# Cheaper conversion of float64 weights and a due time for every piece, in a planned attention, mixture-of-experts and gated-convolution kernel

## The chip, the cores and the metric

One core of one Trainium2 chip runs the whole program. The time is device microseconds (us) of one execution; lower is better. Runs of this kernel agree within about 0.2%.

## The reference

Three layers follow one another, for batch 4, sequence 576 and model width 512 (8 heads of 64). The first is a local attention over a band of seven positions plus an attention on queries, keys and values averaged by four. The second is a causal attention with four experts of which each token takes two. The third is a convolution with five taps that gates a linear product.

```python
out_local = softmax(where(|i-j| < 4, q k^T / 8, -1e9)) v
x = repeat(softmax(qd kd^T / 8) vd, 4) + out_local
for e in range(4):
    ye = softmax(causal(x wq[e] (x wk[e])^T / 8)) (x wv[e]) wo[e]
    x2 += gate[e] * ye
gate = 1 / (1 + exp(-sum_k conv_w[k] * x2[t - 4 + k]))
y = (gate * (x2 w_val)) w_out
```

The weights `w_val`, `conv_w` and `w_out` arrive as float64, since each is float32 data times a float64 scalar. All other inputs are float32.

## The kernel before

Each batch goes through `attention` (four pairs of heads, each with loads, a "down" path on averaged data and two groups of band windows), `project` (keys, queries, values and gate logits of the experts), `experts` (scores, exponentials, weights, transposes and values for five blocks T of 128 tokens and two pairs of experts) and `tail` (the products with `wo`, `w_val` and `w_out`, and the convolution). Products of full precision are sums of three TensorE products of split operands (`mm3`, lines 936 to 939).

Nothing is issued while these functions run. They record pieces: some instructions of one engine with an estimated cost, the buffers that they read and write, and a due time. `Plan.order` (line 174) then plays the pieces through a model of the engines and writes out one order for each of them: on each engine the piece with the least due time among those that are ready goes next, where buffers are to be had. Due times come from `PARAMS` by batch and stage; line 151 adds an entry of `NUDGE`, which is empty. `PARAMS` also says which engine takes many of the pieces (`"v_00": "dve"`), and how many PSUM banks or `row` buffers each use may hold (`c_...`, `r_...`). A PSUM bank (`ps`) that is handed on makes its next writer wait until its last reader is done. The engines work through their queues in the written order, so a piece that has to wait holds up everything behind it on its engine.

The float64 conversion is in `chunk` (line 563). A value of 64 bits is loaded as two 32-bit words; nine chunks go this way: four of `w_val` and four of `w_out`, each of 128 by 512 values, and one of 128 by 20 (`conv_w`). Before, a chunk takes these steps:

- VectorE (DVE) shifts the upper word into float32 place and clears the sign (lines 596 and 600); ScalarE (ACT) takes the upper word's absolute value and its sign (604 and 608); DVE zeroes values that are too small (613).
- DVE shifts the lower word and takes the exponent of the result (619, 620); ACT turns the lower word into a scaled float (624).
- GpSimd (POOL) multiplies the two, adds the product to the value and multiplies by the sign (628 to 630).

Places that the prediction names: the scores of the experts (lines 1085 to 1087), the row minimum of the negated scores on DVE (1111), exponentials on ACT (1119), the weights (1152), transposes (1159), the value product (1220); in the attention the down scores (830), the band scores (872), the transposes (839, 884), products with values (853, 902), the sum of the two paths on DVE (910); the results of the last product leave through line 1315.

Of the kernel before, what the change touches and what calls it, by code (L numbers as in the profile page):

```python
# [21 lines left out]
TINY64 = 2.0 ** -15 * 1.125  # L22

# [6 lines left out]
    8, "c_mo": 3, "c_ms": 2, "c_mt": 3, "c_o": 7, "c_s": 5, "c_t": 4, "c_w": 5, "cv_00": 3, "cv_01": 4,  # L30
# [6 lines left out]
    "pool", "k_23": "dve", "k_30": "pool", "k_31": "dve", "k_32": "pool", "k_33": "pool", "kk_00": "own",  # L37
    "kk_01": "load", "kk_02": "load", "kk_03": "load", "kk_10": "load", "kk_11": "own", "kk_12": "own",
    "kk_13": "load", "kk_20": "load", "kk_21": "own", "kk_22": "load", "kk_23": "load", "kk_30": "load",
    "kk_31": "own", "kk_32": "own", "kk_33": "load", "late": 275.02, "m_000": "dve", "m_001": "dve",  # L40
# [54 lines left out]
}  # L95


NUDGE = {
}

# [201 lines left out]
def f32r(n):  # L302
    return max(0.459 * n, 112) / 1000
# [23 lines left out]
def tile_local_attention__then__moe__then__gated_conv(  # L327
# [14 lines left out]
    nc = tc.nc  # L342
# [1038 lines left out]
```

## Time and profile before

| | |
|---|---|
| median of 3 runs | 431.75 us (431.65 to 432.47) |
| the profiled execution | 431.73 us |
| its span, first to last instruction | 430.0 us |
| busy: PE, PE weight loads | 389.1, 330.0 us |
| busy: DVE, ACT, POOL | 347.0, 287.5, 187.1 us |
| HBM traffic | 81 GB/s over the span |

PE is TensorE's matmul side. An engine is busy while at least one of its instructions runs; the granted clock (PEclk) is 1.00 at 2.4 GHz and 0.50 at 1.2 GHz. Idle time of an engine is named after what ended it. Matmuls overlap in the pipeline, so that a busy PE may still lose small amounts of time between matmuls.

### The profile page before, as it was taken

The numbers are of one execution on the slowest core, as the hardware profiler recorded it, in microseconds if no ns is written. First come the engines' busy times: TensorE is split into PE (matmuls) and PEld (weight loads), VectorE is DVE, ScalarE is ACT, GpSimd is POOL, SyncE is SP. The second block draws the span as 40 slices with busy tenths as digits, with TensorE's granted clock in tenths as the row PEclk, the third lists the DMA queues.
The fourth block names the chain that finished last, engine by engine and source line by source line (L and its number), as shares of the span: only waits on it lengthen the run. The fifth ranks groups of instructions, "written<-read, shape, count | busy, mean of one in ns | idle before, by whom it ended". The sixth has DMA issues, their size and how long they took to land.

```text
span 430.0 us, 10150 instructions
## 1 busy us (share of the span) xinstructions
PE 389.1 (90%) x3520; PEld 330.0 (77%) x3520; DVE 347.0 (81%) x1032; ACT 287.5 (67%) x974; POOL 187.1 (43%) x256
## 2 busy tenths in 40 slices
PE   0856699999789999999988999999999999999996
PEld 0545479877467898797976798979788998878996
DVE  6788848989997869999989999877773667698765
ACT  5485765268778763548989875579898636666541
POOL 8365567377276384357743730210322700134220
PEclk9996779999687999999999999999999999999999
DMA  8897524136422200020355431302101000100111
GB/s 210 228 242 225 141 81 136 31 102 183 134 81 75 80 17 14 0 79 29 111 151 142 142 85 58 100 2 69 36 22 63 2 2 2 37 15 1 48 64 63
DMA packets 28595, 35.45 MB, mean 82 GB/s; under 512 B 3328, under 2 KB 18688, under 8 KB 28544
## 3 DMA queue, kind: packets, MB, share of 16 engines
q1 hardware_dynamic: 28544, 34.81, 28.7%
q8 instruction: 28, 0.46, 0.5%
q14 instruction: 23, 0.19, 0.2%
HBM read 30.08 MB, written 4.72 MB: 81 GB/s over the span
## 4 chain that ended last, share of the span: by engine, by line
PE 51%; DVE 24%; ACT 15%; issue 4%; POOL 3%; DMA 3%; POOLq 0%; DVEq 0%; ACTq 0%
PE ps L937 10%; PE ps L938 10%; PE ps L939 10%; ACT p L786 5%; PE ps L1159 4%; PE ps L1220 4%; PE ps L1085 3%; DMA v<-in_vx_dram 3%; DVE mmin L1111 2%; ACT pT L890 2%; PE ps L902 2%; PE ps L830 2%; DVE pe L1152 2%; DVE pT L890 1%; DVE mpT L551 1%
## 5 line engine op out<-in xcount | busy, mean ns | idle before, releaser
L1275 POOL TENSOR_TENSOR row<-row,row 128x256 f32<-128x256 f32 (+1 forms) x52 | 43.5, 838 | 53.9 <-ACT row L1271 43.6
L1119 ACT ACTIVATE pe<-ps,mmin 128x128 f32<-128x128 f32 (+4 forms) x80 | 41.5, 524 | 18.0 <-DVE mmin L1111 14.8
L786 ACT ACTIVATE p<-ps,mx 128x64 f32<-128x64 f32 (+1 forms) x116 | 39.6, 342 | 10.1 <-DVE mx L781 7.1
L937 PE MATMUL ps<-xh,wqk_h 128*128 128x256 f32 (+1 forms) x128 | 41.4, 323 | 0.6 <-ACT mpT L551 0.2
L1280 DVE SCALAR_TENSOR_TENSOR row<-ps,cw,row 128x320 f32<-128x320 f32 (+1 forms) x76 | 38.0, 515 | 4.3 <-POOL row L1275 3.7
L1152 POOL TENSOR_SCALAR pe<-pe,es,gw 128x384 f32<-128x384 f32 (+3 forms) x23 | 14.5, 631 | 59.9 <-DVE es L1132 26.9
L1111 DVE TENSOR_REDUCE mmin<-ps 128x1 f32<-128x128 f32 (+4 forms) x80 | 35.7, 476 | 5.5 <-PE ps L1087 4.8
L937 PE MATMUL ps<-gh,wout_h 128*128 128x256 f32 (+1 forms) x128 | 39.3, 307 | 0.0
L938 PE MATMUL ps<-gl,wout_h 128*128 128x256 f32 (+1 forms) x128 | 37.9, 296 | 0.0
L1159 PE MATMUL ps<-ident,pe 128*128 128x128 f32 x192 | 34.2, 292 | 4.0 <-DVE row L910 1.9
L938 PE MATMUL ps<-xl,wqk_h 128*128 128x256 f32 (+1 forms) x128 | 37.8, 295 | 0.0
L939 PE MATMUL ps<-xh,wqk_l 128*128 128x256 f32 (+1 forms) x128 | 37.8, 295 | 0.0
L939 PE MATMUL ps<-gh,wout_l 128*128 128x256 f32 (+1 forms) x128 | 37.7, 295 | 0.0
L1159 PEld LDWEIGHTS ps<-ident,pe 128*128 128x128 f32 x192 | 22.2, 146 | 9.6 <-POOL pe L1152 2.3
L830 PE MATMUL ps<-kd,qd 128*112 128x144 f32 x96 | 17.6, 327 | 12.3 <-POOL kd L742 10.7
L1220 PE MATMUL ps<-mpT,vE 128*64 128x320 f32 (+4 forms) x224 | 27.3, 377 | 0.0
L872 PE MATMUL ps<-kz,qz 128*64 128x64 f32 x640 | 25.9, 230 | 0.8 <-DMA kz<-in_kT_dram 0.5
L872 PEld LDWEIGHTS ps<-kz,qz 128*64 128x64 f32 x640 | 22.5, 143 | 4.8 <-issue 2.4
L937 PEld LDWEIGHTS ps<-xh,wqk_h 128*128 128x128 f32 x128 | 24.1, 188 | 2.6 <-issue 0.6
L819 POOL TENSOR_TENSOR p<-p,sm 128x256 f32<-128x256 f32 (+2 forms) x19 | 15.6, 828 | 23.5 <-DVE sm L810 19.2
L1271 ACT ACTIVATE row<-ps,cw 128x256 f32<-128x256 f32 (+1 forms) x52 | 24.6, 499 | 1.5 <-POOL row L1275 0.8
L902 PE MATMUL ps<-pT,vw 128*64 128x116 f32 (+1 forms) x320 | 23.0, 284 | 2.8 <-ACT pT L890 1.7
(195 smaller groups left out, 1327.1 us busy)
## 6 DMA issues: line engine op xcount, KB each, us to landing
vw<-in_vx_dram SPq DMA_DIRECT2D x32, 160.0 KB, 3.7
qz<-in_qT_dram SPq DMA_DIRECT2D x32, 144.0 KB, 3.0
kz<-in_kT_dram SPq DMA_DIRECT2D x32, 144.0 KB, 2.9
v<-in_vx_dram SPq DMA_DIRECT2D x16, 288.0 KB
kt<-in_kT_dram SPq DMA_DIRECT2D x10, 288.0 KB, 5.6
out_dram<-o SPq DMA_DIRECT2D x16, 160.0 KB, 1.8
v<-in_w_val_dram SPq DMA_DIRECT2D x4, 512.0 KB
v<-in_w_out_dram SPq DMA_DIRECT2D x4, 512.0 KB, 3.3
```

Of the source, the lines that this page charges most:

```text
L786: nc.scalar.activation(pv()[:, i], sv()[:, i], AF.Exp, scale=scale, bias=mx.t[:n, i:i + 1], accum_out=sums()[:, i:i + 1])
L872: nc.tensor.matmul(s.t[64 * h:64 * h + 64, (w - w0) * 64:(w - w0) * 64 + 64], qb.t[:, h, WQ * w:WQ * w + 64], kz.t[:, h, WQ * w:WQ * w + 6 ...
L902: nc.tensor.matmul(po.t[64 * h:64 * h + 64, q0 - t0:q1 - t0], vw.t[:, a, 64 * h:64 * h + 64], pT.t[:, a - w0 // 2, h].rearrange("p w q -> ...
L937: nc.tensor.matmul(p, ah, bh, start=first, stop=False)
L938: nc.tensor.matmul(p, ah, bl, start=False, stop=False)
L939: nc.tensor.matmul(p, al, bh, start=False, stop=last)
L1111: nc.vector.tensor_reduce(out=m.t[:, a:a + 1], in_=s.t[:, :c1 - c0], op=ALU.min, axis=AX.X)
L1119: nc.scalar.activation(pe.t[:, c0:c1], s.t[:, :c1 - c0], AF.Exp, bias=m.t[:, 0:1], scale=-1.0, accum_out=es.t[:, a:a + 1])
L1159: nc.tensor.transpose(pt.t[:, (nf - 1 - j) * P:(nf - j) * P], pe.t[:, j * P:(j + 1) * P], ident)
L1220: nc.tensor.matmul(av.t[64 * e:64 * e + 64, z:n], vE.t[:kr, j, 2 * pr + e, :], pT.t[:kr, e, k0:k0 + n - z], start=(j == 0), stop=(j == Tl))
L1275: nc.gpsimd.tensor_add(g.t[:, :nn], g.t[:, :nn], g2.t[:, :nn])
L1280: nc.vector.scalar_tensor_tensor(g.t[:, :nn], x2.t[:, k:k + nn], cw.t[:, m, k:k + 1], g.t[:, :nn], op0=ALU.mult, op1=ALU.add)
```

## The change

A chunk is converted in other steps. DVE copies the sign bit from the upper word into the result with bit operations, so that the sign by ACT and the multiplication by POOL go. The lower word's top 23 bits are placed behind the result's own sign and exponent; POOL subtracts the bare exponent, and DVE scales the difference and adds it. For a chunk, DVE has seven instructions where it had five, ACT one where it had three, POOL one where it had three.

`NUDGE` gets 2,763 entries, one due-time shift for each piece. In `PARAMS` 73 of the letters that place a piece on an engine change, and ten numbers, most of them buffer counts; some constants of the planner's model change too.

```diff
     "a_300": 0, "a_301": 0, "a_310": 0, "a_311": 0, "a_320": 1, "a_321": 1, "a_330": 1, "a_331": 1, "c_d":
-    8, "c_mo": 3, "c_ms": 2, "c_mt": 3, "c_o": 7, "c_s": 5, "c_t": 4, "c_w": 5, "cv_00": 3, "cv_01": 4,
+    6, "c_mo": 6, "c_ms": 2, "c_mt": 2, "c_o": 5, "c_s": 7, "c_t": 4, "c_w": 2, "cv_00": 3, "cv_01": 4,
...
 NUDGE = {
+    0: 0.78, 1: 19.2, 2: -1.61, 3: 0.78, 4: -0.14, 5: -7.62, 6: 16.78, 7: 6.98, 8: 0.76, 9: -21.27, 10:
...
-    PATIENCE, AHEAD, HEAD = 0.1, 4.0, {"dve": 0.13, "pool": 0.05}
+    PATIENCE, AHEAD, HEAD = 0.05, 0.0, {"dve": 0.13, "pool": 0.05}
...
 def f32r(n):
-    return max(0.459 * n, 112) / 1000
+    return max(0.459 * n + 5, 112) / 1000
...
-        raw, a0, a1, ss = buf("v4"), buf("o"), buf("o"), buf("o")
+        raw, a0, a1 = buf("v4"), buf("o"), buf("o")
...
-        @piece("act", act(n, True), [raw, ss], [ss])
-        def _():
-            nc.scalar.activation(ss.t[:, :n], words(1).bitcast(F32), AF.Sign)
-
-        @piece("dve", vec(n), [a0, a1], [f], kind="port")
+        @piece("dve", vec(3 * n, 3, 0) + 0.2, [raw, a0, a1], [f, a0, a1], kind="port")
         def _():
 
             nc.vector.scalar_tensor_tensor(f.t[:, :n], part(1).bitcast(F32), TINY64, part(0).bitcast(F32),
                                            op0=ALU.is_ge, op1=ALU.mult)
-
-
-        @piece("dve", vec(n, 2), [raw, f, a0, a1], [a0, a1], kind="port")
-        def _():
-            nc.vector.tensor_single_scalar(part(0), words(0), 8, op=ALU.logical_shift_right)
-            nc.vector.tensor_single_scalar(part(1), f.t[:, :n].bitcast(I32), 0x7F800000, op=ALU.bitwise_and)
-
-        @piece("act", act(n, True), [a0], [a0])
-        def _():
-            nc.scalar.activation(a0.t[:, :n], part(0), AF.Copy, scale=2.0 ** -44)
-
-        @piece("pool", gps(3 * n, 3), [a0, a1, ss, f], [f, a0])
-        def _():
-            nc.gpsimd.tensor_mul(a0.t[:, :n], a0.t[:, :n], a1.t[:, :n])
-            nc.gpsimd.tensor_add(f.t[:, :n], f.t[:, :n], a0.t[:, :n])
-            nc.gpsimd.tensor_mul(f.t[:, :n], f.t[:, :n], ss.t[:, :n])
+            nc.vector.scalar_tensor_tensor(whole(), words(1), SIGN, whole(), op0=ALU.bitwise_and, op1=ALU.bitwise_or)
+
+            nc.vector.tensor_single_scalar(part(1), whole(), SIGN | 0x7F800000, op=ALU.bitwise_and)
+            nc.vector.scalar_tensor_tensor(part(0), words(0), 9, part(1), op0=ALU.logical_shift_right, op1=ALU.bitwise_or)
+
+        @piece("pool", gps(n), [a0, a1], [a0])
+        def _():
+            nc.gpsimd.tensor_sub(a0.t[:, :n], a0.t[:, :n], a1.t[:, :n])
+
+        @piece("dve", vec(n), [a0, f], [f], kind="port")
+        def _():
+            nc.vector.scalar_tensor_tensor(f.t[:, :n], a0.t[:, :n], 2.0 ** -20, f.t[:, :n], op0=ALU.mult, op1=ALU.add)
         return f
...
-        @piece("dve", 1.66, [L], [ge, gw, gm], kind="port")
+        @piece("dve", 1.9, [L], [ge, gw, gm], kind="port")
```

How instructions move is seen at two places. In the changed kernel a line number is larger by 388 up to the conversion and by 380 behind it (L1159 is L1539, L902 is L1282, L1111 is L1491). `ps_63` is a PSUM bank, `pe_129` a buffer of exponentials, `ah` and `wo` the operands of a product of the tail, `qb`, `kh` and `kl` those of the scores of the last block of tokens.

**First place: PE in batch 0, the transposes of block T = 3 (four matmuls on `pe_129` and `pe_130`).** Before:

```order
L902 MATMUL ps_63<-pT_96,vw_77 64x116 x6
L937 MATMUL ps_69<-kh_118,qb_116 128x288
L938 MATMUL ps_69<-kl_120,qb_116 128x288
L939 MATMUL ps_69<-kh_118,qb_116 128x288
L1098 LDWEIGHTS identb
L1098 MATMUL ps_69<-cmask_160,identb 128x64
L1159 MATMUL ps_63<-ident,pe_129 128x128 x4
L1159 MATMUL ps_70<-ident,pe_130 128x128 x4
```

Now:

```order
L1478 MATMUL ps_70<-cmask_160,identb 128x64
L1317 MATMUL ps_69<-ah_146,wo_h 128x260
L1318 MATMUL ps_69<-al_148,wo_h 128x260
L1319 MATMUL ps_69<-ah_146,wo_l 128x260
L1317 MATMUL ps_69<-ah_146,wo_h 128x260
L1318 MATMUL ps_69<-al_148,wo_h 128x260
L1319 MATMUL ps_69<-ah_146,wo_l 128x260
L1539 MATMUL ps_63<-ident,pe_129 128x128 x4
L1317 MATMUL ps_68<-ah_146,wo_h 128x260
L1318 MATMUL ps_68<-al_148,wo_h 128x260
L1319 MATMUL ps_68<-ah_146,wo_l 128x260
L1539 MATMUL ps_70<-ident,pe_130 128x128 x4
```

Before, the transposes write bank `ps_63`, which the product with values (L902) filled five matmul rows earlier and which DVE must empty (L910) first. Now `ps_63` was last written 38 rows earlier, by transposes of the attention, and products of the tail stand ahead of both groups of transposes.

**Second place: DVE in batch 0, around the row minimum for block T = 2 and the first chunk of `w_out`.** Before:

```order
L791 TENSOR_TENSOR p_93<-ps_63,mx_82 128x384
L735 TENSOR_TENSOR qd_73<-row_99 64x3x48
L1111 TENSOR_REDUCE mmin_132<-ps_69 128x1
L1111 TENSOR_REDUCE mmin_133<-ps_70 128x1
L799 TENSOR_REDUCE ps_63<-p_93 128x6
L596 TENSOR_SCALAR o_152<-v_76 128x512
L1128 TENSOR_SCALAR es_139<-es_139 128x1
```

Now:

```order
L1171 TENSOR_TENSOR p_93<-ps_68,mx_82 128x384
L997 SCALAR_TENSOR_TENSOR o_154<-o_153,o_152 128x512
L999 SCALAR_TENSOR_TENSOR o_154<-v_76,o_154 128x512
L1001 TENSOR_SCALAR o_153<-o_154 128x512
L1002 SCALAR_TENSOR_TENSOR o_152<-v_76,o_153 128x512
L1491 TENSOR_REDUCE mmin_132<-ps_63 128x1
L1491 TENSOR_REDUCE mmin_133<-ps_70 128x1
```

Before, the two row minima (L1111) stand ahead of the conversion; now four of the conversion's instructions (L997 to L1002) stand ahead of them (L1491).

## Rows read from the trace of the kernel before

**Rows 1.** The page's head and its busy times by engine.

```profile
span 430.0 us, 10150 instructions
...
PE 389.1 (90%) x3520; PEld 330.0 (77%) x3520; DVE 347.0 (81%) x1032; ACT 287.5 (67%) x974; POOL 187.1 (43%) x256
```

**Rows 2.** Stretches: us, busy PE PEld DVE ACT POOL (instructions), PEclk, DMA share, GB/s.

```profile
20.00:40.00 20.00, 11.97 (x142) 9.11 (x139) 17.21 (x39) 14.29 (x54) 10.46 (x14) 0.88 1.01 252
...
100.00:120.00 20.00, 17.41 (x151) 11.63 (x150) 18.96 (x69) 15.06 (x64) 9.55 (x15) 0.76 0.54 158
120.00:140.00 20.00, 17.32 (x127) 13.16 (x126) 16.55 (x48) 17.29 (x56) 13.44 (x14) 0.81 0.23 70
...
220.00:240.00 20.00, 16.53 (x204) 13.23 (x204) 18.54 (x54) 19.00 (x77) 7.37 (x9) 1.00 0.54 152
...
420.00:430.00 10.00, 6.41 (x42) 5.88 (x41) 5.40 (x12) 1.86 (x4) 0.15 (x1) 1.00 0.20 67
```

**Rows 3.** Timeline of PE: start, us, instruction, in brackets idle before and releaser.

```profile
10.70 1.78 PE L830 MATMUL ps<-kd,qd 128*112 128x144 f32 x6 [10.70 <-POOL kd L742]
...
108.67 0.45 PE L839 MATMUL ps<-ident,p 112*72 112x112 f32 x3 [1.08 <-ACT mpT L551]
...
113.78 1.24 PE L853 MATMUL ps<-pdT,vd 72*64 72x144 f32 x8 [1.04 <-ACT pe L1119]
...
125.45 1.21 PE L1159 MATMUL ps<-ident,pe 128*128 128x128 f32 x8 [1.86 <-DVE row L910]
...
129.61 1.11 PE L1159 MATMUL ps<-ident,pe 128*128 128x128 f32 x4 [0.71 <-POOL pe L1152]
...
225.71 0.74 PE L839 MATMUL ps<-ident,p 112*72 112x112 f32 x6 [1.38 <-DVE sm L806]
...
229.85 0.41 PE L884 MATMUL ps<-ident,p 128*128 128x128 f32 x2 [1.48 <-ACT pT L890]
```

**Rows 4.** Timeline of DVE just ahead of the idle PE at 125.45.

```profile
124.89 0.50 DVE L910 TENSOR_TENSOR row<-ps,od 128x348 f32<-128x348 f32 x1
```

**Rows 5.** Timeline of PE: the eight matmuls of L853 at the full clock.

```profile
98.98 0.72 PE L853 MATMUL ps<-pdT,vd 72*64 72x144 f32 x8
```

**Rows 6.** Groups by line and shape: busy us, mean ns of one, idle before, releasers.

```profile
L613 DVE SCALAR_TENSOR_TENSOR o<-o,o 128x512 f32<-128x512 f32 x8 | 6.1, 768 | 0.3 <-ACT o L604 0.3
...
L619 DVE TENSOR_SCALAR o<-v 128x512 int32<-128x512 int32 x8 | 3.8, 478 | 0.1
...
L620 DVE TENSOR_SCALAR o<-o 128x512 int32<-128x512 int32 x8 | 4.3, 542 | 0.0
...
L608 ACT ACTIVATE o<-v 128x512 f32<-128x512 f32 x8 | 5.4, 670 | 0.6 <-POOL o L630 0.6
...
L624 ACT ACTIVATE o<-o 128x512 f32<-128x512 int32 x8 | 5.1, 632 | 4.1 <-DVE o L619 4.1
...
L628 POOL TENSOR_TENSOR o<-o,o 128x512 f32<-128x512 f32 x8 | 10.2, 1274 | 16.5 <-ACT o L624 7.9 <-ACT ah L551 6.3 <-DVE ps L799 1.3
L629 POOL TENSOR_TENSOR o<-o,o 128x512 f32<-128x512 f32 x8 | 10.2, 1276 | 0.6
L630 POOL TENSOR_TENSOR o<-o,o 128x512 f32<-128x512 f32 x8 | 10.4, 1304 | 0.6
```

**Rows 7.** Line 596, the conversion's first step: ns min/median/max, first and last start.

```profile
L596 DVE TENSOR_SCALAR o<-v x9: 414/454/1192, 5.0 to 153.5; 128x512 int32<-128x512 int32 x8, 128x20 int32<-128x20 int32 x1
```

**Rows 8.** Groups by line and shape: a piece of which five go to POOL.

```profile
L750 DVE TENSOR_TENSOR v<-v 72x512 f32<-72x512 f32 x13 | 9.9, 762 | 0.7 <-DMA v<-in_vx_dram 0.6
```

**Rows 9.** Timeline of DVE: the same two instructions, without and beside a POOL instruction.

```profile
8.26 0.62 DVE L735 TENSOR_TENSOR qd<-row 64x144 f32<-64x144 f32 x2
...
13.65 1.57 DVE L735 TENSOR_TENSOR qd<-row 64x144 f32<-64x144 f32 x2
```

**Rows 10.** Timeline of POOL, the instruction that ran beside the second of these.

```profile
13.28 1.46 POOL L630 TENSOR_TENSOR o<-o,o 128x512 f32<-128x512 f32 x1
```

**Rows 11.** Timeline at the end: the four last results leave PSUM.

```profile
425.15 1.81 DVE L1315 TENSOR_SCALAR o<-ps 128x320 f32<-128x320 f32 x4 [0.93 <-PE ps L939]
```

More of the change, by code (lines that the diff above doesn't have):

```diff
@@ L22 @@
 TINY64 = 2.0 ** -15 * 1.125
+SIGN = -0x80000000
 PARAMS = {
@@ L33 @@
     "f1": 122.88, "f2": 399.89, "f3": 539.51, "fl0": 8.06, "fl1": 78.77, "fl2": 166.61, "fl3": 48.67,
[3 rows of a table removed]
[L37 to L40, printed above, removed]
[22 rows of a table removed]
@@ L63 @@
-    "dve", "q_02": "pool", "q_03": "dve", "q_10": "pool", "q_11": "pool", "q_12": "pool", "q_13": "pool",
-    "q_20": "dve", "q_21": "dve", "q_22": "pool", "q_23": "dve", "q_30": "dve", "q_31": "pool", "q_32":
-    "dve", "q_33": "dve", "qe_00": "dve", "qe_01": "dve", "qe_10": "dve", "qe_11": "dve", "qe_20": "act",
[5 rows of a table removed]
-    "dve", "v_02": "dve", "v_03": "dve", "v_10": "pool", "v_11": "dve", "v_12": "pool", "v_13": "dve",
-    "v_20": "dve", "v_21": "dve", "v_22": "dve", "v_23": "dve", "v_30": "dve", "v_31": "pool", "v_32":
@@ L73 @@
-    "dve", "v_33": "dve", "ve_0": "dve", "ve_1": "act", "ve_2": "act", "ve_3": "dve", "w_000": "pool",
[12 rows of a table removed]
-    "wl_o": "dve", "wl_out": "pool", "wl_qk": "dve", "wl_vg": "pool", "wq": 826.51, "wt": 25.89, "xl_000":
-    "pool", "xl_001": "pool", "xl_010": "dve", "xl_011": "dve", "xl_020": "pool", "xl_021": "dve",
-    "xl_030": "pool", "xl_031": "dve", "xl_100": "pool", "xl_101": "pool", "xl_110": "pool", "xl_111":
-    "dve", "xl_120": "dve", "xl_121": "pool", "xl_130": "dve", "xl_131": "pool", "xl_200": "dve",
[5 rows of a table removed]
[2 rows of a table added]
@@ new lines @@
+    "pool", "k_11": "pool", "k_12": "pool", "k_13": "pool", "k_20": "pool", "k_21": "dve", "k_22": "pool",
[3 rows of a table added]
+    "own", "kk_32": "own", "kk_33": "load", "late": 275.02, "m_000": "dve", "m_001": "dve", "m_00d":
+    "dve", "m_010": "dve", "m_011": "act", "m_01d": "dve", "m_020": "act", "m_021": "dve", "m_02d": "act",
[20 rows of a table added]
+    "act", "pt_21": "act", "pt_30": "act", "pt_31": "dve", "q_00": "dve", "q_01": "dve", "q_02": "pool",
+    "q_03": "dve", "q_10": "pool", "q_11": "pool", "q_12": "pool", "q_13": "pool", "q_20": "dve", "q_21":
@@ new lines @@
+    "dve", "q_22": "pool", "q_23": "dve", "q_30": "pool", "q_31": "pool", "q_32": "pool", "q_33": "pool",
[7 rows of a table added]
+    "dve", "v_22": "pool", "v_23": "dve", "v_30": "pool", "v_31": "pool", "v_32": "dve", "v_33": "pool",
[12 rows of a table added]
+    "pool", "w_316": "pool", "w_317": "dve", "w_318": "dve", "wl": 207.52, "wl_o": "dve", "wl_out":
+    "pool", "wl_qk": "dve", "wl_vg": "pool", "wq": 826.51, "wt": 25.89, "xl_000": "pool", "xl_001":
+    "pool", "xl_010": "dve", "xl_011": "dve", "xl_020": "dve", "xl_021": "pool", "xl_030": "pool",
@@ L95 @@
+    "xl_031": "dve", "xl_100": "pool", "xl_101": "pool", "xl_110": "pool", "xl_111": "dve", "xl_120":
+    "dve", "xl_121": "pool", "xl_130": "dve", "xl_131": "dve", "xl_200": "dve", "xl_201": "dve", "xl_210":
+    "pool", "xl_211": "pool", "xl_220": "dve", "xl_221": "pool", "xl_230": "dve", "xl_231": "pool",
[4 rows of a table added]
 }
 NUDGE = {
[387 rows of a table added]
 }
@@ L591, in _, with whole @@
             nc.sync.dma_start(out=place(raw.t[:, :2 * n].bitcast(I32)), in_=rows(I32))
-        @piece("dve", vec(n / 2, 1), [raw], [a0, a1, ss], kind="port")
+        def whole():
+            return f.t[:, :n].bitcast(I32)
+        @piece("dve", vec(n, 2), [raw], [a0, a1], kind="port")
         def _():
             nc.vector.tensor_scalar(part(0), words(1), 0x08000000, 3, op0=ALU.bitwise_xor, op1=ALU.logical_shift_left)
-        @piece("dve", vec(n / 2, 1), [a0], [a0], kind="port")
-        def _():
             nc.vector.tensor_single_scalar(part(0), part(0), 0x7FFFFFFF, op=ALU.bitwise_and)
```

481 rows, old and new, of tables (NUDGE, PARAMS) are left out of this document.

## The prediction, as it was put on record

> **What bounds the kernel now.** I read the busy times first. PE is busy 389.1 of 430.0 us and DVE 347.0; no other engine reaches 300 [rows 1]. So PE sets the end, and what can be won is its 40.9 us of idle time and the time it runs at the lower clock. The matmuls themselves stay: PE has the same 2,875 rows in both orders.
>
> Next come the stretches [rows 2]. From 20 to 40 us PE works only 11.97 of 20.00 us while the DMA share is 1.01: 8.03 us of idle time belong to transfers. At the end PE is idle 10.00 - 6.41 = 3.59 us while the last results leave. From 100 to 140 us the granted clock is 0.76 and then 0.81, and 1.00 at 220 to 240. DVE is nearly full where the clock is low: 18.96 of 20.00 us.
>
> Then the timeline of PE [rows 3], which names what its idle time waits for. 10.70 us lie at the head, ended by POOL's `kd`. Six other gaps are shown: 1.08, 1.04, 1.86 and 0.71 between 108 and 130 us, 1.38 and 1.48 at 225 to 230; together 7.55. What is left is 40.9 - 10.70 - 3.59 - 7.55 = 19.06 us in smaller gaps, of which the transfers' 8.03 make 11.03 that an order of work could fill.
>
> The gap of 1.86 ends with L910 on DVE, which starts at 124.89 and takes 0.50 [rows 4]: the transposes L1159 wait for the bank that L910 empties. The 0.71 four us later waits for POOL's weights (L1152). The clock has a price in the same timeline: eight matmuls of L853 take 1.24 us at 113.78 [rows 3], and 0.72 at 98.98 [rows 5], a factor of 1.72 between the lower level (1.2 GHz) and the full one (2.4).
>
> **The change, part by part.**
>
> *The first place (batch 0, T = 3).* The order puts six products of the tail ahead of the transposes and three more between their two groups, and takes the bank's last use 38 rows back. The nearest row for such products: six matmuls of 144 columns took 1.78 us [rows 3], 2.06 ns a column; six of 260 are 3.2 us, or 3.2 / 1.72 = 1.9 if that row stood at the lower clock; three are 1.6 or 0.93. Both cover 1.86 and 0.71. I count both gaps as gone: **-2.57 us**; bounds 0 (the products' own operand `ah`, which comes next if late, holds PE instead) and -2.57. The products were taken from a later place; what they covered there is in the rivals.
>
> *The other shown gaps.* At 113.78 the product L853 waits for exponentials. In the new order what stands before it still reads a bank filled just ahead (L1233, two rows behind its transposes), so I leave 1.04. The two at 225 and 229 stay: there the transposes L1219 (L839 before) stand four rows behind their own scores. The 1.08 at 108.67 waits for an operand's copy on ACT; no reason to count it. Cost 0 for all, bounds -4.98 (1.08 + 1.04 + 1.38 + 1.48) and 0.
>
> *The clock from 100 to 140.* With two levels, 0.76 over 20 us is 2 x 0.24 x 20 = 9.6 us at the lower, and 0.81 is 7.6: 17.2 us, which at full clock would be 17.2 / 1.72 = 10.0. So 7.2 us can come back, and nothing less than 0. PE idles just before and inside this stretch at four places; two of the four go, so I take half: **-3.6 us**.
>
> *The rest of the schedule.* Over the whole of the orders, between the scores of a block and its transposes stood a median of 9 other pieces on PE, now 11, about a fifth more time for the exponentials and weights in between. A fifth of the 11.03 us: **-2.2 us**, bounds 0 and -11.0. The first 40 us are the transfers' (the same 183 of them), and I expect nothing there; at the head PE waits for `kd` behind the same POOL steps, 0.
>
> *The conversion.* On DVE a chunk loses L619 and L620 (478 + 542 ns) and gains three instructions of the form of L613 (768 each) and one like L620 (542) [rows 6]: +2,846 - 1,020 = +1.83 us, for eight wide chunks +14.6. The narrow ninth is left out, being 20 columns of 512. The masking forms are new. As bounds I take 478 ns, the shortest row of the pass, hence 8 x (3 x 0.478 + 0.542 - 1.020) = +7.7, and 1,192 ns, the longest L596 [rows 7], hence +24.8. ACT loses 670 + 632 a chunk, 10.4 in all; POOL loses two of three steps, 1,274 + 1,304, 20.6 in all. The chain of a chunk behind L613 was 0.478 + 0.542 + 0.632 + 3.854 = 5.5 us and becomes 0.768 + 0.542 + 0.768 + 1.276 + 0.768 = 4.1; chunks start from 5.0 to 153.5 us [rows 7] and their users are the products of the tail, so this latency is hidden by the experts' work between. Against the +14.6 on DVE stand the new letters: about 40 pieces fewer on DVE, other than the conversion. A large one costs 762 ns (L750) [rows 8], so at most 30.5 us leave; I take half, 15, since many are smaller. DVE's total is then unchanged. Its cover is DVE's own idle time, 83 us in all; where that is gone, between 100 and 120, see the slower rival. **0 us**, bounds -3 and +7.3.
>
> Two DVE instructions L735 show what POOL's share matters for: 0.62 us at 8.26, 1.57 at 13.65 [rows 9], where POOL was inside L630 from 13.28 for 1.46 [rows 10]. This speaks for the conversion's shorter POOL part; its gain is inside the bound of -3 and not in the sum. The Trainium skill, "SBUF — State Buffer", section "SBUF: two separate sides", says more: a DVE instruction with two SBUF inputs and a GpSimd instruction exclude each other for a whole instruction. The two rows fit it to 0.14 us (POOL's rest of 1.09 and then 0.62 would be 1.71). By that rule what a chunk costs is the time that both together hold the ports: 1.83 - 2.58 = -0.75 us a chunk, -6.0 for eight, and the time would be 417 rather than 423.
>
> *What costs nothing.* The planner's constants and costs change only the order. The last four results still leave through L1315, 1.81 us [rows 11], behind the last matmuls, so the 3.59 stay.
>
> **Sum.** -2.57 - 3.6 - 2.2 + 0 = -8.4. The profiled execution took 431.73, 1.73 more than its span, and stands within 0.02 of the median of 431.75. 431.73 - 8.4 = 423.3, forecast **423 us**.
>
> **The rivals.**
>
> *More is filled.* The clock stays full from 100 to 140 (-7.2), the two gaps go (-2.57) and between half and all of the 11.03 (-5.5 to -11.0): -15.3 to -20.8, hence 416 to 411, the middle 414. For it: nearly three thousand shifts loosen every stage. Against: DVE is at 18.96 of 20 in this stretch, and gains DVE work ahead of it.
>
> *The stalls only move.* The tail's products now cover T = 3 and leave a hole of 2.57 where they stood; the clock falls as before. Then 431.7, within 0.2%, which is about what a measurement of this kernel can tell from no change. For it: DVE's total work is as large as before. Against: the PE order shows longer covers at many places. That the order doesn't change at all is excluded by the two places shown.
>
> *Slower: DVE becomes the bound at the chunks of `w_out`.* Four of the conversion's instructions now stand ahead of the row minima of T = 2 (second place), and PE can do nothing with T = 2 until exponentials and weights have followed. The four chunks of `w_out` bring 4 x 1.83 = 7.3 us to DVE between 100 and 155 us. It decides if what is added exceeds DVE's idle time there, 1.04 + 3.45 = 4.49 us [rows 2], and the pieces that leave DVE leave elsewhere. With nothing won it gives 431.7 + 7.3 = 439. Against: ACT and POOL have idle time there and take pieces over.
>
> **How the numbers follow.** Forecast 0.54, more filled 0.25, stalls only move 0.07, slower 0.14. The range goes from 411, the end of the second case, to 434, part of the way into the slower one; left out is the larger part of the slower case and a rest below, some 0.16. Faster by over 0.2% is the first two, 0.79; same 0.07; slower 0.14.
>
> **What would show it.** The profile after should have PE's idle time down from 40.9 to about 36, no gap ended by L910's successor (L1290) or by the weights at T = 3, and a granted clock of about 0.9 in the two stretches; the gaps at 225 to 230 still there; the new DVE instructions of 128x512 near 768 ns. If those take over 1 us, the conversion costs more than I took. If the clock is full from 100 to 140, the second case is right; if PE's gaps there end with DVE's row minima (L1491), the slower one. I am wrong in kind if most of the gain lies before 40 us, where I expect none.

## The result, and the profile after

The changed kernel takes 437.17 us (436.60 to 437.24, 3 runs) against 431.75 (431.65 to 432.47): a ratio of 1.0116, interval 1.0096 to 1.0136. It is slower by 5.4 us where 8.4 less were forecast. The 0.2% given for the agreement of runs is too narrow: 77 executions of the kernel before, those that accompanied the experiments, lie between 429.27 and 434.35 us, so what follows goes by ratios and their 95% intervals.

The page's head and busy times of the changed kernel:

```profile
span 435.5 us, 10087 instructions
...
PE 391.9 (90%) x3520; PEld 331.5 (76%) x3520; DVE 344.0 (79%) x1017; ACT 282.8 (65%) x968; POOL 184.1 (42%) x263
```

Against [rows 1], PE's idle time (span less busy) went up, from 40.9 to 43.6, and PE was busy 2.8 us longer with the same matmuls. DVE lost 3.0 us in all, as the prediction's balance wanted. Where it lost them is seen when the span is cut at 160 us. Two stretches of the kernel before (us; busy PE, PEld, DVE, ACT, POOL with instructions; PEclk, DMA share, GB/s):

```profile
0.00:160.00 160.00, 128.25 (x1168) 101.29 (x1169) 129.29 (x371) 105.11 (x357) 97.09 (x141) 0.89 0.48 131
160.00:430.00 270.00, 260.86 (x2354) 228.74 (x2352) 217.71 (x662) 182.38 (x618) 89.97 (x116) 1.00 0.18 54
```

The same two of the changed kernel:

```profile
0.00:160.00 160.00, 127.06 (x1143) 98.77 (x1144) 136.31 (x375) 99.70 (x349) 80.37 (x126) 0.89 0.53 131
160.00:430.00 270.00, 262.87 (x2367) 230.97 (x2367) 207.67 (x644) 181.37 (x615) 103.72 (x138) 1.00 0.18 51
```

DVE has 7.0 us more to do in the first 160 us, where nearly all of the conversion, most of PE's idle time (before, 31.75 of 40.9 us) and all of its low clock lie, and 10.0 less behind it, where PE is busy 97% of the time anyway. POOL is the mirror of it: 16.7 less, then 13.8 more. The mean clock of the first stretch is 0.89 in both.

Stretches of the changed kernel, to be read against [rows 2]:

```profile
20.00:40.00 20.00, 15.50 (x146) 12.48 (x146) 14.36 (x35) 14.04 (x50) 10.26 (x14) 0.66 1.01 212
40.00:60.00 20.00, 15.41 (x109) 11.14 (x109) 15.18 (x38) 11.02 (x39) 14.02 (x18) 0.68 0.54 144
60.00:80.00 20.00, 18.82 (x188) 15.99 (x187) 17.59 (x41) 10.13 (x31) 9.05 (x11) 0.97 0.40 115
...
100.00:120.00 20.00, 16.23 (x182) 11.99 (x180) 17.81 (x63) 15.21 (x67) 11.25 (x18) 0.89 0.69 175
120.00:140.00 20.00, 15.96 (x123) 11.91 (x121) 18.98 (x53) 17.25 (x58) 8.33 (x9) 0.94 0.20 59
140.00:160.00 20.00, 18.68 (x169) 15.14 (x166) 19.54 (x49) 13.65 (x38) 10.56 (x13) 1.00 0.22 70
```

Two stretches of the kernel before that [rows 2] don't hold:

```profile
40.00:60.00 20.00, 15.92 (x133) 12.17 (x132) 13.29 (x32) 14.27 (x51) 14.29 (x17) 0.69 0.39 110
...
140.00:160.00 20.00, 19.14 (x165) 17.01 (x164) 14.62 (x39) 13.80 (x36) 12.39 (x13) 1.00 0.14 44
```

**The clock moved.** At two levels, time at the lower one is 2 x (1 - PEclk) x 20. Before, that is 4.8 + 12.4 + 9.6 + 7.6 = 34.4 us; after, 13.6 + 12.8 + 1.2 + 4.4 + 2.4 = 34.4. From 100 to 140 it fell from 17.2 to 6.8, more than was forecast, and between 20 and 80 it rose by as much. That the two sums are equal is chance, for single executions differ by more: w1 of experiment 5, which has the old order and takes as long as the kernel before, has 48.0 us at the lower level, much of it here:

```profile
20.00:40.00 20.00, 15.02 (x145) 11.62 (x144) 15.32 (x38) 13.65 (x51) 10.22 (x14) 0.64 0.95 237
```

**DVE filled up:** from 120 to 160 us it is busy 38.52 of 40 us, where it was 31.17.

The gaps of PE that answer to [rows 3], in the changed kernel's timeline (start, us, instruction; in brackets idle before and releaser):

```profile
11.08 0.82 PE L1210 MATMUL ps<-kd,qd 128*112 128x144 f32 x2 [11.08 <-POOL kd L1122]
...
108.13 1.39 PE L1252 MATMUL ps<-kz,qz 128*64 128x64 f32 x40 [0.59 <-DVE row L1290]
...
113.47 0.48 PE L1219 MATMUL ps<-ident,p 112*72 112x112 f32 x3 [1.35 <-ACT pe L1499]
...
116.48 0.66 PE L1539 MATMUL ps<-ident,pe 128*128 128x128 f32 x2 [0.63 <-DVE mx L1161]
...
117.92 0.69 PE L1539 MATMUL ps<-ident,pe 128*128 128x128 f32 x2 [0.79 <-POOL pe L1532]
...
126.36 0.55 PE L1539 MATMUL ps<-ident,pe 128*128 128x128 f32 x3 [1.14 <-ACT mpT L939]
...
132.07 0.63 PE L1539 MATMUL ps<-ident,pe 128*128 128x128 f32 x4 [1.27 <-DVE pe L1532]
...
134.40 0.77 PE L1219 MATMUL ps<-ident,p 112*72 112x112 f32 x6 [0.57 <-ACT mpT L939]
135.33 0.61 PE L1282 MATMUL ps<-pT,vw 128*64 128x116 f32 x8 [0.17 <-DVE row L1660]
...
139.52 0.50 PE L1465 MATMUL ps<-kh,qh 64*128 64x512 f32 x2 [0.70 <-DVE row L1672]
...
235.76 0.47 PE L1233 MATMUL ps<-pdT,vd 72*64 72x144 f32 x4 [1.79 <-DVE sm L1186]
```

At the first place the bank that L910 emptied is no longer waited for: the first transposes of T = 3 start at 129.84 right behind the tail's products. But the second group of T = 3 waits 1.27 us at 132.07 for weights, which now come from DVE, and the block before it 1.14 at 126.36 for ACT's copy out of its bank. DVE's timeline shows what stands around there:

```profile
124.57 0.68 DVE L1010 SCALAR_TENSOR_TENSOR o<-o,o 128x512 f32<-128x512 f32 x1
125.28 0.69 DVE L1491 TENSOR_REDUCE mmin<-ps 128x1 f32<-128x512 f32 x1
```

The conversion's last step stands in front of a row minimum whose exponentials, weights and transposes follow one another. The four waits of 1.35, 0.79, 1.14 and 1.27 make 4.55 us, where [rows 3] had 4.69 between 108 and 130 and the timeline of before shows no other up to 142. But the changed kernel has five more (0.59, 0.63, 0.57, 0.17, 0.70), four of them ended by results of DVE; all nine make 7.21, and PE's idle time from 100 to 140 us rose from 5.27 to 7.81.

The conversion itself is as large as forecast (groups by line and shape, wide chunks only):

```profile
L999 DVE SCALAR_TENSOR_TENSOR o<-v,o 128x512 int32<-128x512 int32 x8 | 6.6, 820 | 0.3
L1010 DVE SCALAR_TENSOR_TENSOR o<-o,o 128x512 f32<-128x512 f32 x8 | 6.2, 777 | 0.9 <-POOL o L1006 0.9
L1002 DVE SCALAR_TENSOR_TENSOR o<-v,o 128x512 int32<-128x512 int32 x8 | 6.1, 764 | 0.3
L997 DVE SCALAR_TENSOR_TENSOR o<-o,o 128x512 f32<-128x512 f32 x8 | 6.1, 762 | 0.0
...
L988 DVE TENSOR_SCALAR o<-o 128x512 int32<-128x512 int32 x8 | 4.8, 599 | 0.3
L987 DVE TENSOR_SCALAR o<-v 128x512 int32<-128x512 int32 x8 | 3.8, 479 | 2.4 <-DMA v<-in_w_val_dram 2.4
L1001 DVE TENSOR_SCALAR o<-o 128x512 int32<-128x512 int32 x8 | 3.4, 427 | 0.3
```

The four added instructions take 820 + 777 + 764 + 427 = 2,788 ns a chunk, where the prediction had 2,846.

### The profile page after: what moved, and what is told of

Read it like the earlier page. It is cut to its first block, busy times and chain, and to the rows that moved or that the text cites. A ratio compares the mean times of both kernels' runs of the same rounds, so it can differ in the third digit from the quotient of the medians.

```text
span 435.5 us, 10087 instructions
## 1 busy us (share of the span) xinstructions
PE 391.9 (90%) x3520; PEld 331.5 (76%) x3520; DVE 344.0 (79%) x1017; ACT 282.8 (65%) x968; POOL 184.1 (42%) x263
## 4 chain that ended last, share of the span: by engine, by line
PE 61%; DVE 19%; DMA 7%; ACT 5%; POOL 3%; issue 3%; SPq 1%; POOLq 0%; ACTq 0%; DVEq 0%
PE ps L1317 14%; PE ps L1318 12%; PE ps L1319 12%; PE ps L1539 4%; PE ps L1465 4%; PE ps L1600 4%; PE ps L1252 2%; PE ps L1210 2%; DMA kt<-in_kT_dram 2%; PE ps L1282 2%; DVE row L1290 1%; DMA vw<-in_vx_dram 1%; DMA o<-in_wvg_dram 1%; PE ps L1219 1%; DMA o<-in_wo_dram 1%
## 5 line engine op out<-in xcount | busy, mean ns | idle before, releaser
L1317 PE MATMUL ps<-xh,wqk_h 128*128 128x256 f32 (+1 forms) x128 | 42.3, 331 | 0.2
L1491 DVE TENSOR_REDUCE mmin<-ps 128x1 f32<-128x512 f32 (+4 forms) x80 | 36.6, 476 | 5.5 <-PE ps L1467 4.7
L1539 PE MATMUL ps<-ident,pe 128*128 128x128 f32 x192 | 32.1, 281 | 5.5 <-DVE pe L1532 1.9
L1210 PE MATMUL ps<-kd,qd 128*112 128x144 f32 x96 | 19.2, 348 | 13.2 <-POOL kd L1122 12.4
L1252 PE MATMUL ps<-kz,qz 128*64 128x64 f32 x640 | 27.1, 238 | 2.9 <-DMA kz<-in_kT_dram 1.4
L1252 PEld LDWEIGHTS ps<-kz,qz 128*64 128x64 f32 x640 | 23.5, 150 | 8.0 <-issue 3.5
L1539 PEld LDWEIGHTS ps<-ident,pe 128*128 128x128 f32 x192 | 22.1, 142 | 8.9 <-POOL pe L1532 1.9
L1210 PEld LDWEIGHTS ps<-kd,qd 128*112 128x112 f32 x96 | 15.6, 216 | 16.3 <-POOL kd L1122 13.0
L1199 POOL TENSOR_TENSOR p<-p,sm 128x256 f32<-128x256 f32 (+2 forms) x23 | 17.8, 780 | 23.3 <-DVE sm L1190 14.2
```

What stands on the lines that cost most here:

```text
L1210: nc.tensor.matmul(s.t[:112, t * SD:(t + 1) * SD], qd.t[:, t, :], kd.t, start=True, stop=True)
L1252: nc.tensor.matmul(s.t[64 * h:64 * h + 64, (w - w0) * 64:(w - w0) * 64 + 64], qb.t[:, h, WQ * w:WQ * w + 64], kz.t[:, h, WQ * w:WQ * w + 6 ...
L1317: nc.tensor.matmul(p, ah, bh, start=first, stop=False)
L1491: nc.vector.tensor_reduce(out=m.t[:, a:a + 1], in_=s.t[:, :c1 - c0], op=ALU.min, axis=AX.X)
L1539: nc.tensor.transpose(pt.t[:, (nf - 1 - j) * P:(nf - j) * P], pe.t[:, j * P:(j + 1) * P], ident)
```

## The experiments

A change of this kind has two halves, the conversion and the order (table, letters, counts). All experiments keep the queues of every engine as one of the two kernels has them, except where they say otherwise. Ratios are to runs of the kernel before on the same chip (medians of 431.5 to 432.6).

**1. Each conversion in the other order.** In the old order the new steps stand in the old places, the last one right behind POOL's subtraction; in the new order the reverse.

```diff
-            nc.scalar.activation(ss.t[:, :n], words(1).bitcast(F32), AF.Sign)
...
+            nc.gpsimd.tensor_sub(a0.t[:, :n], a0.t[:, :n], a1.t[:, :n])
+            nc.vector.scalar_tensor_tensor(f.t[:, :n], a0.t[:, :n], 2.0 ** -20, f.t[:, :n], op0=ALU.mult, op1=ALU.add)
```

> The kernel before, every engine's queue as it stood, with the conversion's new instructions in the old places. Theory 'conversion' (the seven DVE instructions are what costs): 435 to 438 us, about that of the changed kernel. Theory 'start' (the order of the first 80 us is what costs, 3.6 to 4.8 us by the two traces): 431.7 within 1. Theory 'spread' (small losses all along the new order): 431.7 within 1 too. By the port rule weighed in the prediction, 6 us less: 426.

> The changed kernel, every queue as it stands, with the old conversion's instructions in the places of the new. Theory 'conversion': back to 431 to 433 us. Theories 'start' and 'spread': 437 within 1.5, with a little more where the longer POOL part comes late.

Measured 442.93 us (1.0246, interval 1.0190 to 1.0303) and 446.79 (1.0339, 1.0282 to 1.0395). Neither theory foresaw that both exchanges cost: 11 us one way, 9.6 the other. What an exchange costs includes the places that the moved steps were given. For f1 experiment 3 separates that; for f2, where the scaling on ACT stands in the place of POOL's step, no run does.

**2. Each order for the first 80 us of the other.** Pieces that one order starts in its first 80 us come first, in that order; the rest follows in the other (the order is given as a list, and a piece goes in once its buffers are free).

```diff
-                        if p.due[0] > queue[i][1].due[0] + (PARAMS["stick"] if e == "pe" else self.AHEAD):
+        rank = {p: POS[n] for p, n in number.items()}
+        ready = sorted((rank[p], number[p]) for p in self.pieces if not waiting[p])
```

> The new order for what it starts in its first 80 us, the old order for all the rest; new conversion throughout. Theory 'start': 431.7 + 3.6 to 4.8 = 435 to 437 us, and a low granted clock between 20 and 40 us. Theory 'spread': half or less of the loss, 432 to 434. Theory 'conversion': 436 or so, as for any order. The seam at 80 us may add about 1.

> The old order for what it starts in its first 80 us, the new order for all the rest; new conversion throughout. Theory 'start': 437.2 - 3.6 to 4.8 = 432 to 434 us, and the full clock between 20 and 35 us. Theory 'spread': 435 to 436. Theory 'conversion': 437. The seam at 80 us may add about 1.

Measured 443.70 (1.0260, 1.0216 to 1.0305) and 446.02 (1.0317, 1.0270 to 1.0365), both above both kernels. The seam costs far more than the 1 us allowed. With the old start, this stretch behind the seam has PE idle for 4.95 us (the changed kernel: 0.88):

```profile
80.00:100.00 20.00, 15.05 (x123) 11.76 (x122) 14.38 (x47) 6.49 (x29) 6.87 (x8) 0.91 0.23 61
```

So these two tell nothing of the start.

**3. The conversion well placed, smaller, and halved.** In the old order, f1b puts the last step 2.2 us later in the planned queue; m2 does scale and add on POOL instead. The halved conversions (b1 in the old, a1 in the new order) leave out sign and lower word.

```diff
-            nc.vector.scalar_tensor_tensor(f.t[:, :n], a0.t[:, :n], 2.0 ** -20, f.t[:, :n], op0=ALU.mult, op1=ALU.add)
+            later.append((plan.at + 0.555 * gps(3 * n, 3), lambda: nc.vector.scalar_tensor_tensor(
+                f.t[:, :n], a0.t[:, :n], 2.0 ** -20, f.t[:, :n], op0=ALU.mult, op1=ALU.add)))
```

For m2, and for a1 (b1 is alike, in the old steps):

```diff
+            nc.gpsimd.tensor_scalar_mul(a0.t[:, :n], a0.t[:, :n], 2.0 ** -20)
+            nc.gpsimd.tensor_add(f.t[:, :n], f.t[:, :n], a0.t[:, :n])
```

```diff
-            nc.vector.scalar_tensor_tensor(whole(), words(1), SIGN, whole(), op0=ALU.bitwise_and, op1=ALU.bitwise_or)
...
-            nc.gpsimd.tensor_sub(a0.t[:, :n], a0.t[:, :n], a1.t[:, :n])
...
-            nc.vector.scalar_tensor_tensor(f.t[:, :n], a0.t[:, :n], 2.0 ** -20, f.t[:, :n], op0=ALU.mult, op1=ALU.add)
```

> The new conversion in the old order once more, with the last DVE step put behind POOL's subtraction (2.2 us later in the queue for a wide chunk), so that DVE doesn't stand and wait for POOL. Theory 'DVE time' (the added instructions cost what they take, since DVE's queue is full where chunks are converted): 441 to 443, about as before this edit (442.9). Theory 'DVE waits' (what cost was DVE's waiting for POOL in that place, 4.5 us in the trace, and what stood behind it): 434 to 437.

> The new conversion in the old order with its last step (scale and add) on POOL as two instructions: six DVE instructions a chunk where the old had five, POOL three as the old, no wait of DVE on POOL. Added to DVE are 8 x (2 x 0.768 + 0.542 - 1.020) = 8.5 us where the whole new conversion adds 14.6. Theory 'DVE time': 431.9 + 11 x 8.5 / 14.6 = 438. Theory 'DVE waits': 432 to 434.

> The kernel before with only the upper word converted: sign and lower word are left out (on DVE the shift and the exponent, on ACT sign and scaling, on POOL all three steps). Theory 'old conversion is covered': 430 to 432, since POOL's 3.85 us and ACT's 1.3 us a chunk lie beside other work. Theory 'old conversion costs': 426 to 429.

> The changed kernel with only the upper word converted: sign and lower word are left out (four DVE instructions of 2.8 us a chunk and POOL's subtraction). Its distance to 437.2 is what the new conversion's added part costs in its own order; its distance to the kernel before with the same left out is what the new order is worth alone. Theory 'DVE time': 427 to 430 (some 8 us less), and the orders are then alike. Theory 'order': 434 to 437, 4 or more above the old order with the same left out.

Measured: f1b 437.08 (1.0087, 1.0062 to 1.0112), m2 436.42 (1.0075, 1.0046 to 1.0104), b1 428.37 (0.9896, 0.9862 to 0.9930), a1 431.42 (0.9973, 0.9946 to 1.0000). f1b lies 0.1 us above the range of its theory 'DVE waits', b1 where 'old conversion costs' has it; m2 and a1 lie between their two theories. These four carry the answer:

- **The new conversion costs about 4 us in the old order** (f1b: 3.8 by the ratio, 4.5 by the medians), nearly as much as the whole change. Of the first experiment's 11 us, 6 to 7 went with the place of the last step alone, at which DVE stood and waited for POOL. The step was placed by hand in an order made for the old conversion, so the 4 us can hold some misfit too; no run plans the old letters anew for the new steps.
- **The new order brings no gain.** With the new conversion it stands at 1.0116 against f1b's 1.0087, and the intervals overlap; with the halved one it is slower, 431.4 against 428.4.
- Per wide chunk DVE's steps take 1.8 us (b1: L596, L600, L613), 2.8 (before), 4.0 (m2) and, by the rows of the changed kernel, 4.6 (f1b); the time is 428.4, 431.9, 436.4, 437.1. It rises with every step: 8.7 us for 8 x 2.8 = 22.4 us of DVE time, about 0.4 us per us. In the new order 437.2 - 431.4 = 5.8 us for the same 22.4, about 0.26. This is no price of DVE time alone: b1 also drops steps of ACT and POOL, and v1 (experiment 6), with b1's three DVE instructions, takes 430.27.

In f1b PE is busy as long as before, and its idle time rose from 40.9 to 436.1 - 388.9 = 47.2 us:

```profile
PE 388.9 (89%) x3520; PEld 329.6 (76%) x3520; DVE 360.5 (83%) x1050; ACT 279.5 (64%) x956; POOL 167.6 (38%) x238
```

From 100 to 160 us, where `w_out` is converted, PE idles 6.13 us in the kernel before, 9.13 in the changed one, 9.89 in f1b and 5.35 in a1. The stretch of f1b, and that of a1:

```profile
100.00:160.00 60.00, 50.11 (x418) 37.40 (x414) 55.33 (x162) 42.18 (x149) 26.70 (x34) 0.89 0.32 100
```

```profile
100.00:160.00 60.00, 54.65 (x473) 42.17 (x472) 49.90 (x149) 48.86 (x180) 24.21 (x30) 0.91 0.33 96
```

One wait can be followed from one kernel to the other, that for the bank which L910 empties (L917 in f1b): 1.86 us before, 1.87 in b1 and in v1 of experiment 6, 2.35 in m2 and, in f1b,

```profile
131.10 1.21 PE L1166 MATMUL ps<-ident,pe 128*128 128x128 f32 x8 [2.94 <-DVE row L917]
```

Before, DVE reached the two row minima of this block ahead of PE and waited for the scores; in f1b, with more of the conversion ahead of them, it doesn't wait there. The first line is of the kernel before, the second of f1b:

```profile
118.96 1.29 DVE L1111 TENSOR_REDUCE mmin<-ps 128x1 f32<-128x512 f32 x2 [0.65 <-PE ps L1087]
```

```profile
124.42 1.27 DVE L1118 TENSOR_REDUCE mmin<-ps 128x1 f32<-128x512 f32 x2
```

The wait alone is not the price: in h1 (experiment 5) and in the relief of DVE (experiment 4), which take about as long as the kernel before, it is 2.43 and 2.52.

In the two stretches of a1, DVE has 17.2 us less to do than in the changed kernel in the first 160 us, and PE is busy 3.25 us longer there.

```profile
0.00:160.00 160.00, 130.31 (x1186) 102.46 (x1187) 119.12 (x353) 104.13 (x374) 72.47 (x118) 0.90 0.50 133
160.00:430.00 270.00, 260.49 (x2337) 229.47 (x2335) 201.78 (x630) 178.54 (x595) 101.54 (x136) 0.99 0.17 53
```

**4. DVE time added alone, the letters alone, and a relief of DVE.** In the kernel before, groups of four instructions on a scratch tile, early (one group in each wide chunk) or late (eight from 200 us on); the 73 letters alone, on top of f1b; and two letters that send the low halves of `wqk` and `wo` to POOL.

```diff
+        for _ in range(4):
+            nc.vector.scalar_tensor_tensor(spare, spare, 0.5, spare, op0=ALU.mult, op1=ALU.mult)
```

```diff
-    "wl_o": "dve", "wl_out": "pool", "wl_qk": "dve", "wl_vg": "pool", "wq": 826.51, "wt": 25.89, "xl_000":
+    "wl_o": "pool", "wl_out": "pool", "wl_qk": "pool", "wl_vg": "pool", "wq": 826.51, "wt": 25.89, "xl_000":
```

> The kernel before, with 32 added DVE instructions on a scratch tile that nobody else reads or writes (128x384 floats, about 0.58 us each by the pace of L613, some 18 us in all), four behind L613 of each wide chunk, where the new conversion also adds its work. Theory 'place' (DVE time costs where chunks are converted, in the first 160 us): slower by 4 to 7 us, 436 to 439. If only the longer chain of a chunk, or POOL's part, had cost: within 1 of before.

> The kernel before with the same 32 instructions, in eight groups of four at planned times from 200 us on, 18 us apart. Theory 'place': within 0.5 us of before, though DVE's busy total is as large as in the early case. Theory 'total' (the balance of the prediction, which counted DVE time alike wherever it lies): 436 to 439 as in the early case.

> The new conversion in the old order with its last step placed late (437.1 measured), and the 73 new letters, each piece at its old place among the others. By the prediction's balance, the pieces that leave DVE pay for the conversion: 432 to 433. Theory 'place': counted by the old order and the planner's costs, DVE loses only some 4 us net in its first 160 us, the rest after it where PE doesn't wait: 435 to 437, and pieces of a slower engine may cost some of that again.

> The kernel before, every piece at its old place, with the low halves of wqk (four DVE instructions of 0.79 us between 37 and 47 us) and of wo (two of 0.68 between 20 and 27 us) subtracted on POOL. Theory 'place': DVE gets 4.5 us in the stretch in which the conversion's added time cost a third of itself, so 1 to 2 us faster, 430 to 431. If POOL's longer steps (about 1.3 us each) come late for the first products: 432 to 434.

Measured 444.84 (1.0313, 1.0276 to 1.0350), 458.26 (1.0580, 1.0530 to 1.0631), 447.58 (1.0364, 1.0325 to 1.0404) and 431.93 (1.0016, 0.9994 to 1.0038). Every theory missed its time, only the last by no more than 0.1 us (POOL's longer steps come late, 432 to 434). The theory that only early DVE time counts falls: late groups cost twice as much as early ones, 26.4 against 13.0 us, for scratch work of 20.5 and 19.5 us. One of them in the timeline of DVE, and what PE waits for behind it:

```profile
254.62 3.78 DVE L571 SCALAR_TENSOR_TENSOR spare<-spare 128x384 f32<-128x384 f32 x4
258.32 0.51 DVE L920 TENSOR_TENSOR row<-ps,od 128x348 f32<-128x348 f32 x1
```

```profile
258.88 0.64 PE L947 MATMUL ps<-ah,wo_h 128*128 128x324 f32 x1 [3.48 <-DVE row L920]
```

A group that stands in front of a result that PE needs soon passes on nearly its whole length. This speaks for a price of DVE instructions that is set by what stands behind them in the queue, not by the busy share of the stretch. The letters alone cost 10.5 us on top of f1b; that pieces on other engines need other places is the likely reason, which no run separates. And 4.5 us taken from DVE between 20 and 47 us gained nothing.

**5. The load buffer.** SP's waits named one load buffer `v`, with all loads queued behind it. By instruction and releaser, total, times, longest, in the kernel before:

```profile
SPq L691 <- DVE o L619: 30.7, 5, 11.2
```

And with the new conversion in the old order (f1b):

```profile
SPq L698 <- DVE o L627: 36.2, 6, 12.0
```

So u1 and u2 free `v` sooner (the lower word is left out, its place taken by other data), h1 holds it longer with a tiny reader, w1 reads the lower word first.

```diff
-            nc.vector.scalar_tensor_tensor(part(0), words(0), 9, part(1), op0=ALU.logical_shift_right, op1=ALU.bitwise_or)
+            nc.vector.scalar_tensor_tensor(shaped(part(0)), other.bitcast(I32), 9, shaped(part(1)),
+                                           op0=ALU.logical_shift_right, op1=ALU.bitwise_or)
```

For h1 and for w1:

```diff
+            if n == 512:
+                later.append((plan.at + 1.8, lambda: nc.vector.tensor_copy(spare[:, :2].bitcast(I32), raw.t[:, 0:2].bitcast(I32))))
...
+            nc.vector.tensor_single_scalar(f.t[:, :n].bitcast(I32), words(0), 8, op=ALU.logical_shift_right)
+            nc.vector.scalar_tensor_tensor(a0.t[:, :n], part(1).bitcast(F32), TINY64, part(0).bitcast(F32),
+                                           op0=ALU.is_ge, op1=ALU.mult)
```

> The new conversion in the old order with its last step placed late (437.1 measured), but its sixth instruction takes the lower word from the identity matrix instead of the loaded words, at the same size; so the lower word is left out of the value, and the load buffer v is free after the sign instruction, 1.3 us sooner, with no less work on any engine. Theory 'load buffer' (there is one v; SP's queue stands until its last reader on DVE is done, and all later loads behind it; the new conversion reads it three instructions long where the old read it one): 432.5 to 434.5. Theory 'DVE time': 437 within 1.

> The changed kernel with the same one edit (lower word left out of the value, v free 1.3 us sooner). Theory 'load buffer': 433.5 to 436, less gain than in the old order where the new order loads differently. Theory 'DVE time': 437 within 1.

> The kernel before with one more reader of v for each wide chunk: DVE copies two words a partition (about 0.06 us) some 1.3 us behind the shift that was v's last reader, so v is held as long as by the new conversion while nothing else changes. Theory 'load buffer': 435 to 437. Theory 'DVE time': 432.5 at most.

> The kernel before with the old conversion's shift of the lower word put ahead of the masking of small values (results kept in other buffers, as many instructions), so that v is free 0.7 to 1 us sooner in each chunk. Theory 'load buffer': 1 to 2 us faster than before, about 430.5. Theory 'DVE time': within 0.5 of before.

Measured 436.07 (1.0105, 1.0076 to 1.0134), 436.76 (1.0109, 1.0076 to 1.0142), 432.51 (1.0019, 0.9990 to 1.0048) and 431.58 (1.0006, 0.9978 to 1.0034). All four lie where 'DVE time' has them, u1 and h1 at the edge of it: by the medians the load buffer is worth about 1 us at most, by h1's interval 2, and it is not what makes the change 5 us slower.

**6. Where the cost lies, and a faster version.** v1 is the kernel before without the lower word but with the sign; a1w halves the conversion for `w_val` alone.

```diff
-            nc.vector.tensor_single_scalar(part(0), words(0), 8, op=ALU.logical_shift_right)
-            nc.vector.tensor_single_scalar(part(1), f.t[:, :n].bitcast(I32), 0x7F800000, op=ALU.bitwise_and)
...
-            nc.gpsimd.tensor_mul(a0.t[:, :n], a0.t[:, :n], a1.t[:, :n])
-            nc.gpsimd.tensor_add(f.t[:, :n], f.t[:, :n], a0.t[:, :n])
             nc.gpsimd.tensor_mul(f.t[:, :n], f.t[:, :n], ss.t[:, :n])
```

And for a1w, ahead of the sign instruction, POOL's step and the last step:

```diff
+            if src is w_val:
+                return
```

> The kernel before with the lower word left out of the conversion and the sign kept: DVE loses the shift and the exponent, ACT the scaling, POOL two of three steps; a weight then has the 20 mantissa bits of its upper word, about one part in a million. Theory 'DVE time' (a microsecond of DVE in a chunk costs about 0.4 us: 8.7 us lie between 3 and 7 DVE instructions a chunk, 22 us of DVE time): 431.9 - 0.4 x 8.1 = 428.5 to 429.5, faster than both kernels. If POOL's chain or the lost ACT step had been what the half conversion saved: 430.5 to 432.

> The changed kernel with sign and lower word left out for the four chunks of w_val alone (those converted before 80 us); w_out's four are converted in full. With all eight halved it took 431.4, with none 437.2. Theory 'DVE time, alike per chunk': 434.3. If the first 80 us, where the new order loses 3.6 to 4.8 us to the old, carry the conversion's cost: 432 to 433. If w_out's chunks between 100 and 155 us carry it (the slower rival of the prediction): 436 to 437.

a1w took 436.31 (1.0112, 1.0074 to 1.0150), hardly below the changed kernel; halving `w_out`'s four as well (a1) takes off another 4.9. **By the times, in the new order the conversion's cost goes with the chunks of `w_out`**, between 100 and 160 us. The 4.9 is the price of sign and lower word together, not of what the change adds to them, and `w_out` halved alone was not run. The trace of a1w doesn't bear the times out: with `w_out` converted in full, PE idles only 6.11 us from 100 to 160, and 41.4 in all where the changed kernel has 43.6, but it is busy 3.1 us longer, at a lower clock (44.4 us at the lower level against 34.4). So what the first four chunks gave may have been spent on the clock, and their share stays open.

```profile
PE 395.0 (91%) x3520; PEld 334.6 (77%) x3520; DVE 331.3 (76%) x1001; ACT 283.9 (65%) x968; POOL 178.3 (41%) x259
```

```profile
100.00:160.00 60.00, 53.89 (x481) 41.87 (x479) 56.42 (x164) 46.66 (x162) 30.15 (x36) 0.89 0.35 102
```

```profile
0.00:160.00 160.00, 128.19 (x1137) 100.24 (x1137) 123.08 (x357) 99.58 (x346) 73.08 (x120) 0.87 0.52 131
```

v1 took 430.27 (0.9958, 0.9938 to 0.9978). It beats both kernels, with weights of 20 mantissa bits where the reference's have more. By the ratio it saves 1.8 us, less than the 2.4 to 3.4 that 'DVE time' expects, and its time is next to the other theory's 430.5 to 432. b1, with the same DVE instructions and without ACT's sign and POOL's last step, saves 4.5 by its ratio, so part of the old conversion's cost lies on ACT and POOL.

## Why the prediction was wrong

- **The conversion, "0 us", failed.** Its size was right: +14.6 on DVE forecast, (2,788 - 1,020) x 8 = 14.1 by these rows. The relief came too: DVE's total fell by 3.0, so 17.1 us left where 15 were taken. What failed is the step from "DVE's total is then unchanged" to 0 us. It was a balance over the whole span, with the relief behind 160 us (-10.0) and the load ahead of it (+7.0), and it didn't ask what stands behind the added instructions in DVE's queue. The new conversion costs about 4 us in the old order, in the profiled execution all of it idle time of PE; in the new order sign and lower word together cost 5.8. The bound of +7.3 held it.
- **The first place, -2.57, failed.** The wait for L910's bank went as argued, and the tail's products covered the first group. But the second group's 0.71 became 1.27, 1.14 came at 126.36, and further waits opened on both sides: 7.21 us of shown waits for 4.69. So the stalls didn't only move, as the second rival has it; they grew. Two are of the kind that the prediction said should be gone: 0.59 at 108.13 ends with L1290, 1.27 with the weights of T = 3.
- **The clock, -3.6, failed.** Its local part came true: 17.2 us of low clock became 6.8, by the prediction's factor worth 10.4 x (1 - 1 / 1.72) = 4.4 us. In the profiled execution 10.4 us came back between 20 and 80 us, where the prediction expected nothing. That this belongs to the new order isn't shown, since w1 has it in the old one. And the factor overprices low clock: w1 has 13.6 us more of it than the kernel before, by the factor 5.7 us, and its profiled execution took 433.29 us, 1.6 more.
- **The rest of the schedule, -2.2, failed.** Longer covers in PE's order did not bring less idle time: 43.6 for 40.9. Counted in pieces, a cover says nothing of when the covered work begins.
- **The slower rival came nearest to the mechanism.** It named `w_out`'s chunks, DVE between 100 and 155 us and 439 us; 437.2 came. DVE's idle time from 100 to 140 fell from 4.49 only to 3.21 us, but from 120 to 160 it fell from 8.83 to 1.48. PE's idle time from 100 to 160 rose by 3.0 us in the changed kernel and by 3.8 in f1b. Its sign, gaps that end with the row minima (L1491), didn't come: they end with copies, weights and other results behind them. That 439 is so near is partly luck: it put 7.3 us on `w_out`'s four chunks, where f1b has about 4 for all eight. It got a chance of 0.14, since ACT and POOL were to take pieces over; DVE had 6.2 us more to do from 100 to 160 all the same.
- **The port rule** (the Trainium skill, "SBUF — State Buffer", section "SBUF: two separate sides") would have given 6 us less for the conversion. In the old order, where nothing else changes, it costs about 4 more, so this is not what the conversion's price goes by here. That the two engines do slow each other is shown below.

What stays open: how the 4 us split among single waits and between `w_val` and `w_out`, how much of them is misfit of the order, and why PE was busy 2.8 us longer in the changed kernel. The runs show that the time rises with the conversion's instructions on DVE, and that the load buffer is not the cause; v1 against b1 shows that the old conversion's cost is not DVE's alone.

## What to carry to other kernels

Price an instruction added to an engine by what stands behind it in the queue and who waits for that, here a row minimum, its exponentials and PE's transposes. A balance of busy time doesn't do it, neither over the span nor by stage: 4.5 us taken from DVE early gained nothing, and work added late, where PE had little idle time, cost more than its own length. Half of a change put into an order made for the other half measures the misfit too, so place the moved step with care, or take its work away in both orders and compare those. And when a clock or a gap improves in one stretch, sum the same quantity over the whole span, and look at it in a second execution, before counting it.

## What the runs showed of the hardware

The time at the lower clock, summed over the span, says little of a kernel's time here: 34.4 us in the profiled execution of the kernel before (431.73 us) and 48.0 in that of w1 (433.29 us). The scratch groups of the late case in experiment 4 show DVE slowed beside POOL: four instructions took 2.34 us at 210.60, where POOL was idle from 209.67 to 214.00, and 3.78 at 254.62, beside four POOL instructions between 254.28 and 257.98. Freeing the one load buffer 1.3 us sooner, with SP in wait for it over 30 us in all, changed the time by about 1 us at most (u1 against f1b).
